# A fused attention and SwiGLU kernel: the order of its first transfers, clears and moves is changed

## The chip, the cores and the metric

The kernel runs on one core of a Trainium2 chip. The metric is the device time of one launch in microseconds (us). A core has a matrix engine (TensorE, PE in the profile, with its weight loads shown apart as PEld), VectorE (DVE), ScalarE (ACT), GpSimd (POOL) and SyncE (SP), which here only issues transfers. Each engine works through its own list of instructions in order and waits on semaphores. Transfers (DMAs) are issued from an engine's queue; SP and ACT issue all of them in this kernel.

## The reference

`x` is 2048 rows of 576 numbers in bf16. The result is `x` plus an attention branch plus a gated feed-forward branch, both fed by the same layer norm:

```python
xn = layernorm(x)                                 # over the 576 columns
q, k, v = split(xn @ wqkv)                        # 32 heads of 18 columns
s = where(0 <= i - j < 256, q @ k.T * 18**-0.5, -1e9)
attn = (softmax(s) @ v) @ wo
ffn = (silu(xn @ w1) * (xn @ w3)) @ w2            # 4608 wide
out = x + attn + ffn
```

## The kernel before

The 2048 rows are worked in four chunks (`c`) of 512. A chunk has projections (q, k, v), then 36 units (`u`), then a second stage of `w2` and `wo` products with the residual sum. A unit makes 128 of the 4608 hidden columns for the chunk's 512 rows: nine steps (`n`) of a pair of matmuls (`unit_pairs`, line 704), one for w3 and one for w1, each over 64 rows of contraction in half of the array, then a tanh on ScalarE (`unit_tanh`) and two products on VectorE (`unit_h`). Between the pairs of chunk 0's and the later chunks' units the score steps of the attention are spread (`spaced_step`, line 1020): a pair of score matmuls or more, an exp on ScalarE and masks on GpSimd. The product with v (`pv`) comes in unit 14 (for chunk 0) and later; its results are divided (`o_scale`), turned on VectorE (`o_turn`) and carried to their rows by transfers (`o_pack`, `o_rest`). `JOBS` are three pairs of PSUM banks, dealt in turn by `job()` to units, projections and `pv`: a unit's pair comes up again three deals later.

Every operation is recorded by `add` with the buffers it reads (`r`), writes first (`w`) or joins in writing (`j`); the waits between engines are worked out from these keys. Within an engine the program's order is the order of execution.

The prologue (line 809 on) loads the four x tiles of 128 rows that make chunk 0. Tiles 0 and 3 go on SP's queue, 1 and 2 on ACT's (`load_x`), then the weights of v (`wv`) and of q and k (`wa`). VectorE clears `oq` with zeros (line 821), and the zeros are multiplied by themselves on PE (`warm`, line 825), ten matmuls of 512 columns, before there is real work. Tile 0 is normalized (`ln_stats`, `ln_apart`), turned by PE into PSUM (`xn_turn`, line 399: five blocks of two 64-row halves) and moved by ScalarE into `xnT` (line 413), 640 columns at once. `proj_begin` and `proj_end` issue the two parts of a projection: a part begins with `n` = 0, 1, ... over the blocks of `xnT`. The turn of tile 1 stands between the parts of v 0, and so on. Tile 3's sum and sum of squares are taken by ScalarE (`act_sum`) instead of VectorE.

SP's queue carries, in the program's order: the first feed-forward weights (`load_w13`, six parts fill one of the slots that four units use), the swap of row halves `xnS` (`xn_swap`), four more weight parts, the key rows of head groups 0 and 1 (`span_main(0, 2)`, `span_last(0, 2)`), two transfers of query rows for groups 2 to 7 (`span_main(2, G, "sp", slice(0, 2))`), and then, unit by unit, weight parts that are owed (`owe_part`: after pairs 3, 6 and 8 of units 0 to 3, after pairs 3 and 8 later), the key rows of groups 2 to 7 in three large transfers (after unit 1), their tails (`span_last(2, G, ...)`: one after unit 2, three after unit 4, three after unit 5) and the x tiles of chunk 1 (`loads`, ahead of units 6, 8 and 17). Two of the second slot's six weight parts go on ACT's queue. The statistics of chunk 1's first tile stand on VectorE after unit 13.

All pairs of a unit name `xnS` among what they read, though only pairs 4 to 7 take their moving rows from it:

```python
src = xnT[r0:r0 + 64, c % 2, k // 2, :] if n in (0, 1, 2, 3, 8) else xnS[r0:r0 + 64, n - 4, :]
...
r=[("w13", sl), "xnS"] + xk(c), **{"j" if n else "w": [("ps", b0 + r)]})
```

Of the kernel before, what the change touches and what calls it, by code (L numbers as in the profile page):

```python
# [5 lines left out]
dt = mybir.dt  # L6
# [158 lines left out]
def bass_parallel_sum__sliding_block__glu_gated_swiglu__prompt_kernel(  # L165
# [17 lines left out]
    CH = 512  # L183
# [14 lines left out]
    with ExitStack() as es:  # L198
# [95 lines left out]
        def load_x(t, eng="sp"):  # L294
            nonlocal xp_ctr
            s = xp_ctr % NXP
            xp_ctr += 1
            add(eng, lambda e: e.dma_start(xp[s][:], x2[t * 128:(t + 1) * 128, :]), w=[("xp", s)], dma=f"xp{s}")
            return s
# [99 lines left out]
        def xn_turn(t, banks, eng="dve"):  # L399
            i = t % 2  # L400
            c, tt = divmod(t, TB)
            for k in range(5):
                for r in range(2):
                    r0 = 64 * r
                    bv = half_bank(banks[r])[:, 64 * k:64 * k + 64]
                    add("pe", lambda e, bv=bv, r0=r0, k=k: e.transpose(  # L406
                        bv, xn[i][r0:r0 + 64, k * 128:(k + 1) * 128], ident[r0:r0 + 64, r0:r0 + 64],
                        tile_position=(r0, 0)),
                        r=[("xn", i), "ident"] + ([("xnd", i)] if k == 4 else []), **{"j" if k else "w": [("ps", banks[r])]})
            both = PS[:, banks[0]:banks[0] + 2, :].bitcast(dt.bfloat16)  # L410
            src = both[:, :, 0:320].rearrange("p r (k f) -> p k r f", f=64)
            dst = xnT[:, c % 2, :, tt * 128:(tt + 1) * 128].rearrange("p k (r f) -> p k r f", f=64)
            move = (lambda e: e.tensor_copy(dst, src)) if eng == "dve" else (lambda e: e.activation(dst, src, ACT.Copy))  # L413
            add(eng, move, r=[("ps", b) for b in banks], w=[("xnT", c % 2, tt)])
# [15 lines left out]
        def xk(c):  # L430
            return [("xnT", c % 2, tt) for tt in range(TB)]
# [6 lines left out]
        def proj_part(c, what, banks, part, behind=()):  # L438
# [3 lines left out]
            for n in range(5 - part):  # L442
                for r in range(2):
# [8 lines left out]
                    elif kind == "8":  # L452
                        out_ = PS[:, banks[x], 0:CH // 2]
                        st, mv = wp[rows, kd, i, :], xnT[rows, c % 2, kd, x * (CH // 2):(x + 1) * (CH // 2)]
                        keys = ["wpr", "wp0", "wp1"] + xk(c)
                    else:
                        out_ = PS[:, banks[x], 0:HD]
                        st, mv = xnT[rows, c % 2, kd, i * 128:(i + 1) * 128], wv[rows, kd, x * HD:(x + 1) * HD]
                        keys = ["wvd" if n == 4 else f"wv{n // 2}", ("xnT", c % 2, i)]
# [195 lines left out]
        def o_scale(i):  # L655
# [5 lines left out]
                r=uq_keys[i] + ["rden", "oq0"], w=["oq"])  # L661

        def o_turn(g, half):
            i = g // 2 % NOD
            c0 = half * (CH // 2)
            add("dve", lambda e: e.transpose(od[i][:, g % 2, c0:c0 + CH // 2], oq[:, c0:c0 + CH // 2]),  # L666
                r=["oq", "oq0"], **{"j" if half or g % 2 else "w": [("od", i)]})
# [36 lines left out]
        def unit_pairs(c, u, n0, n1, b0):  # L704
# [3 lines left out]
            for n in range(n0, n1):  # L708
                for r in range(2):
# [6 lines left out]
                        r=[("w13", sl), "xnS"] + xk(c), **{"j" if n else "w": [("ps", b0 + r)]})  # L716
# [93 lines left out]
        add("act", lambda e: e.activation(sm[:, 3:4], eps[:], ACT.Sqrt), r=["eps"], w=[("sm", 3)])  # L810
        for t in (0, 3, 1, 2):
            xslot[t] = load_x(t, "act" if t > 1 else "sp")
# [8 lines left out]
        add("dve", lambda e: e.memset(oq[:].bitcast(dt.float32), 0.0), w=["oq0"])  # L821

        add("dve", lambda e: e.memset(qv[:, 0:2, :].bitcast(dt.float32), 0.0), w=[("q", g) for g in range(2)])

        def warm(b, *widths):
            for k, w in enumerate(widths):
                add("pe", lambda e, w=w: e.matmul(PS[:, b, 0:w], oq[:, 0:128], oq[:, 0:w], start=True, stop=True),  # L827
                    r=["oq0"], **{"j" if k else "w": [("ps", b)]})

        warm(4, *[CH] * 10)  # L830
# [109 lines left out]
        for what in [("q", 0), ("q", 1), ("q", 2), ("q", 3), ("8", 7), None]:  # L940
# [5 lines left out]
            elif got == ("q", 0):  # L946
                load_w13((), 4)
                span_main(0, 2, "act")
            elif got == ("q", 2):
                load_w13((), 2, "act")  # L950
# [3 lines left out]
        span_main(2, G, "sp", slice(0, 2))  # L954
# [6 lines left out]
        for c in range(NC):  # L961
# [7 lines left out]
            if c == 0:  # L969
                loads[6] = (0, 1)  # L970
# [75 lines left out]
            for u in range(NF):  # L1046
# [7 lines left out]
                for n in range(9):  # L1054
                    into = nxt - (clock + 9 - n)
                    if (u, n) == JOINT[c]:
# [24 lines left out]
                        later(u + 2, lambda g=g, ja=ja: (o_turn(g + 1, 1), o_pack(ja, "sp"), o_scale(2)))  # L1081
                        later(u + 3, lambda g=g: (o_turn(g + 2, 0), o_turn(g + 2, 1), o_scale(3)))
                        later(u + 3, lambda kept=kept: free.extend(kept))
                        later(u + 4, lambda g=g: o_turn(g + 3, 0))
                        later(u + 5, lambda g=g, ja=ja: (o_turn(g + 3, 1), o_pack(ja + 1, "sp")))
                    if (c == 0 or u or n > 1) and 9 * u + n not in calm and done < len(att) and (free or done < len(early) or done in held) and (clock >= nxt or (n == 8 and into < 3 and clock >= soon)):
# [8 lines left out]
                if u == FIRST[c]:  # L1095
# [10 lines left out]
                    later(u + 3, lambda j=j: (o_turn(2 * j + 1, 1), o_pack(j, "sp")))  # L1106
                    if j == 0:
                        for n in range(7):
                            later(u + 4 + (n if c == 0 else n // 2 + n // 6), lambda n=n: o_rest(n, "sp" if c else "act"))
# [12 lines left out]
                if c == 0 and u == 1:  # L1122
                    span_main(2, G, "act", slice(2, None))
                if c == 0 and u == 2:
                    span_last(2, G, slice(0, 1))
                if c == 0 and u in (4, 5):
                    span_last(2, G, slice(1, 3) if u == 4 else slice(3, None))
# [83 lines left out]
```

## Time and profile before

| | us |
|---|---|
| three runs | 557.55, 557.74, 560.05 |
| median | 557.74 |
| the profiled execution, its own time | 558.27 |
| the span of its instructions | 556.5 |
| TensorE's share of the span | 99% |
| granted clock over the span, as the records have it | 1.000 |

The profile is of one execution. Its busy times count work alone: issuing a transfer or waiting is not counted. A row of the timeline has the start, the time, the engine (SPq and ACTq are queues of transfers), the line of the code, the operation, and what is written from what; merged rows have a count and run from the first start to the last end. In brackets stands the idle time before it and what ended it. A row of groups has busy time and mean ns of one. A row of DMA issues has the KB of each and the median time from issue to landing; q1 is SP's queue and q10 ACT's in this kernel. A row of the chain of waits has start, time and what was on the chain. A row of stretches has the stretch, its length, each engine's busy time with its number of instructions (PE, PEld, DVE, ACT, POOL), the clock, the DMA share and GB/s.

### The profile page before, as it was taken

The numbers are of one execution on the slowest core, as the hardware profiler recorded it, in microseconds if no ns is written. First come the engines' busy times: TensorE is split into PE (matmuls) and PEld (weight loads), VectorE is DVE, ScalarE is ACT, GpSimd is POOL, SyncE is SP. The second block draws the span as 40 slices with busy tenths as digits, with TensorE's granted clock in tenths as the row PEclk, the third lists the DMA queues.
The fourth block names the chain that finished last, engine by engine and source line by source line (L and its number), as shares of the span: only waits on it lengthen the run. The fifth ranks groups of instructions, "written<-read, shape, count | busy, mean of one in ns | idle before, by whom it ended". The sixth has DMA issues, their size and how long they took to land.

```text
span 556.5 us, 15754 instructions
## 1 busy us (share of the span) xinstructions
PE 552.4 (99%) x6772; PEld 349.6 (63%) x6772; DVE 311.1 (56%) x583; ACT 259.9 (47%) x359; POOL 162.7 (29%) x385
## 2 busy tenths in 40 slices
PE   8999999999999999999999999999999999999998
PEld 4676554677654545677766544747776554455776
DVE  6466979610366888851046687874105577678211
ACT  6457766100287774700038787550005777756000
POOL 6423534300034452530003454333000334333000
PEclk9999999999999999999999999999999999999999
DMA  9986999777367459676726639677572673633652
GB/s 246 200 166 166 218 179 197 153 203 182 94 140 154 126 123 182 174 176 177 199 61 139 160 110 174 144 188 177 154 187 54 138 174 107 165 108 103 164 150 65
DMA packets 127216, 85.96 MB, mean 154 GB/s; under 512 B 34451, under 2 KB 124907, under 8 KB 127147
## 3 DMA queue, kind: packets, MB, share of 16 engines
q1 hardware_dynamic: 125107, 83.09, 64.9%
q10 hardware_dynamic: 2040, 1.87, 1.4%
q8 instruction: 53, 0.87, 0.7%
q14 instruction: 16, 0.13, 0.1%
HBM read 71.29 MB, written 2.36 MB: 132 GB/s over the span
## 4 chain that ended last, share of the span: by engine, by line
PE 99%; ACT 0%; DVE 0%; issue 0%
PE ps L713 50%; PE ps L785 25%; PE ps L461 10%; PE ps L587 6%; PE ps L644 3%; PE ps L792 3%; PE ps L827 1%; PE ps L699 0%; PE ps L406 0%; ACT xnT L413 0%; DVE ofin L803 0%; DVE oq L821 0%
## 5 line engine op out<-in xcount | busy, mean ns | idle before, releaser
L713 PE MATMUL ps<-xnT,w 64*128 64x512 bf16 x1400 | 186.2, 376 | 0.0
L713 PE MATMUL ps<-xnS,w 64*128 64x512 bf16 x1120 | 154.5, 376 | 0.0
L785 PE MATMUL ps<-w,hT 128*128 128x288 bf16 x1156 | 146.7, 286 | 0.0
L728 DVE SCALAR_TENSOR_TENSOR gs<-th,ps 128x512 bf16<-128x512 bf16 x144 | 97.8, 679 | 76.8 <-ACT th L722 75.9
L785 PEld LDWEIGHTS ps<-w,hT 128*128 128x128 bf16 x1156 | 112.5, 98 | 28.9 <-issue 0.2
L713 PEld LDWEIGHTS ps<-xnT,w 64*128 64x128 bf16 x1400 | 74.6, 94 | 58.6 <-issue 0.5
L722 ACT ACTIVATE th<-ps 128x512 bf16<-128x512 f32 x144 | 85.6, 595 | 45.1 <-PE ps L713 42.7
L731 DVE SCALAR_TENSOR_TENSOR hT<-gs,ps 128x512 bf16<-128x512 bf16 x144 | 98.9, 687 | 5.0
L713 PEld LDWEIGHTS ps<-xnS,w 64*128 64x128 bf16 x1120 | 59.7, 94 | 45.4
L596 ACT ACTIVATE pt<-ps 128x1024 bf16<-128x1024 f32 (+1 forms) x70 | 70.7, 1010 | 31.4 <-PE ps L587 31.1
L474 ACT ACTIVATE stage<-ps 128x512 bf16<-128x512 f32 x16 | 9.5, 596 | 142.0 <-PE ps L461 142.0
L623 POOL TENSOR_TENSOR hT<-hT,mk 128x128 int32<-128x128 int32 (+1 forms) x59 | 24.0, 429 | 171.4 <-ACT hT L596 171.2
L803 DVE TENSOR_TENSOR ofin<-ps,xp 128x288 bf16<-128x288 f32 x31 | 13.3, 455 | 108.3 <-PE ps L699 58.1
L623 POOL TENSOR_TENSOR pt<-pt,mk 128x128 int32<-128x128 int32 (+1 forms) x124 | 49.9, 427 | 28.8 <-ACT pt L596 28.8
L587 PE MATMUL ps<-qv,kv 64*128 64x320 bf16 (+4 forms) x528 | 53.3, 260 | 0.0
L587 PEld LDWEIGHTS ps<-qv,kv 64*128 64x128 bf16 x528 | 27.7, 94 | 26.2 <-ACT hT L596 1.5
L461 PE MATMUL ps<-xnT,wp 64*128 64x512 bf16 (+1 forms) x360 | 38.1, 355 | 0.0
L596 ACT ACTIVATE w<-ps 128x1024 bf16<-128x1024 f32 (+1 forms) x32 | 32.3, 1010 | 12.2 <-PE ps L587 12.1
L596 ACT ACTIVATE hT<-ps 128x1024 bf16<-128x1024 f32 (+1 forms) x32 | 32.3, 1009 | 5.3 <-PE ps L587 4.8
L623 POOL TENSOR_TENSOR w<-w,mk 128x128 int32<-128x128 int32 (+1 forms) x56 | 22.9, 429 | 28.7 <-ACT w L596 28.7
L666 DVE STREAM_TRANSPOSE od<-oq 128x256 bf16<-128x256 bf16 x64 | 25.8, 427 | 6.9 <-POOL oq L659 6.9
L461 PEld LDWEIGHTS ps<-xnT,wp 64*128 64x128 bf16 x360 | 18.9, 94 | 14.6 <-ACT stage L474 0.3
(93 smaller groups left out, 384.0 us busy)
## 6 DMA issues: line engine op xcount, KB each, us to landing
w<-in_B_w_dram SPq DMA_DIRECT2D x208, 192.0 KB, 4.1
w<-in_B_w_dram SPq DMA_DIRECT2D x72, 288.0 KB, 3.3
xp<-in_A_x_dram SPq DMA_DIRECT2D x30, 144.0 KB, 3.0
out_dram<-ofin SPq DMA_DIRECT2D x31, 72.0 KB, 1.7
xnS<-xnT SPq DMA_DIRECT2D x8, 256.0 KB, 4.2
oT<-od SPq DMA_DIRECT2D x40, 36.0 KB
pt<-in_A_wqkv_dram SPq DMA_DIRECT2D x4, 288.0 KB, 5.6
hT<-in_B_w_dram SPq DMA_DIRECT2D x6, 192.0 KB, 3.6
```

The source lines that it names most:

```text
L461: op = add("pe", lambda e, out_=out_, st=st, mv=mv, n=n, r0=r0, first=first: e.matmul(out_, st, mv, start=first, stop=(part == 1 and n == ...
L587: add("pe", lambda e, r0=r0, out_=out_, kb=kb, q0=q0, nb=nb: e.matmul(out_, kb4[r0:r0 + 64, g, kb + NV - NB, :] if kb < 0 else kv[r0:r0 + ...
L596: add("act", lambda e: e.activation(pt_slot(sl)[:, 0:w, :], PS[:, SC[0]:SC[1] + 1, 0:w].rearrange("p r q -> p q r"), ACT.Exp, scale=scale) ...
L623: add("pool", lambda e, vb=vb, mm=mm: e.tensor_tensor(vb, vb, mm, ALU.mult), r=(key if n == 0 else []) + ["mk"], **{"w" if n == 0 else "j" ...
L644: add("pe", lambda e, p=p, q=q, pr=pr, sl=sl, g=g, pos=pos, q0=q0, nb=nb, col=col, first=first, n=n: e.matmul(PS[32 * q:32 * q + VW, banks ...
L666: add("dve", lambda e: e.transpose(od[i][:, g % 2, c0:c0 + CH // 2], oq[:, c0:c0 + CH // 2]), r=["oq", "oq0"], **{"j" if half or g % 2 els ...
L713: op = add("pe", lambda e, n=n, r0=r0, r=r, k=k, src=src: e.matmul(PS[:, b0 + r, :], wt[r0:r0 + 64, k, fl * 128:(fl + 1) * 128], src, star ...
L722: add("act", lambda e: e.activation(th[i][:], PS[:, bg, :], ACT.Tanh, scale=0.5), r=[("ps", bg)], w=[("th", i)])
L728: add("dve", lambda e: e.scalar_tensor_tensor(out=gs[i][:], in0=th[i][:], scalar=1.0, in1=PS[:, bg, :], op0=ALU.add, op1=ALU.mult), r=[("t ...
L731: add("dve", lambda e: e.scalar_tensor_tensor(out=hT[:, u, :], in0=gs[i][:], scalar=0.5, in1=PS[:, bu, :], op0=ALU.mult, op1=ALU.mult), r= ...
L785: add("pe", lambda e: e.matmul(bank, hT[:, f, tt * 128:(tt + 1) * 128], w2[sl][:, k, n0:n1], start=first, stop=(c + 1 == NC and half == 1 ...
L792: add("pe", lambda e: e.matmul(bank, oT[:, k, tt * 128:(tt + 1) * 128], wo[:, k, d0 + n0:d0 + n1], start=False, stop=(k == 3 and (half == ...
```

## The change

- The clear of `oq` is made in two parts, 64 and 192 columns (counted as 32-bit numbers), and stands ahead of the x loads in the program. The warming matmuls wait for the first part alone and read only its columns, repeated; there are nine and a half instead of ten. The x tiles on ACT's queue wait for the second part.
- The move of tile 0's turned rows is made in two parts, blocks 0 and 1 and then 2 to 4 (new key `xnT0`); the matmuls of v 0 with `n` over 1 wait for the second part, those with `n` 0 and 1 only for the first.
- A unit's pairs wait for `xnS` only in pairs 4 to 7.
- All six weight parts of the second slot go on SP, ahead of the keys of groups 0 and 1. Queries and keys of groups 2 to 7 go on SP together after unit 3, their tails after units 4, 5 and 6, and the first x tiles of chunk 1 ahead of unit 7 instead of unit 6.
- The packs of the attention's rows (`o_pack`, `o_rest`) are each issued a unit later than before, or later in the same unit's list.
- No score step is put ahead of pair 7 of unit 22 of chunk 0; it comes at the next place where one may.

```diff
@@ -291,11 +291,11 @@
 
         xp_ctr = 0
 
-        def load_x(t, eng="sp"):
+        def load_x(t, eng="sp", behind=()):
             nonlocal xp_ctr
             s = xp_ctr % NXP
             xp_ctr += 1
-            add(eng, lambda e: e.dma_start(xp[s][:], x2[t * 128:(t + 1) * 128, :]), w=[("xp", s)], dma=f"xp{s}")
+            add(eng, lambda e: e.dma_start(xp[s][:], x2[t * 128:(t + 1) * 128, :]), r=list(behind), w=[("xp", s)], dma=f"xp{s}")
             return s
 
         nfill = 0
@@ -408,10 +408,12 @@
                         tile_position=(r0, 0)),
                         r=[("xn", i), "ident"] + ([("xnd", i)] if k == 4 else []), **{"j" if k else "w": [("ps", banks[r])]})
             both = PS[:, banks[0]:banks[0] + 2, :].bitcast(dt.bfloat16)
-            src = both[:, :, 0:320].rearrange("p r (k f) -> p k r f", f=64)
-            dst = xnT[:, c % 2, :, tt * 128:(tt + 1) * 128].rearrange("p k (r f) -> p k r f", f=64)
-            move = (lambda e: e.tensor_copy(dst, src)) if eng == "dve" else (lambda e: e.activation(dst, src, ACT.Copy))
-            add(eng, move, r=[("ps", b) for b in banks], w=[("xnT", c % 2, tt)])
+            for n, (k0, k1) in enumerate(((0, 2), (2, 5)) if t == 0 else ((0, 5),)):
+                src = both[:, :, 64 * k0:64 * k1].rearrange("p r (k f) -> p k r f", f=64)
+                dst = xnT[:, c % 2, k0:k1, tt * 128:(tt + 1) * 128].rearrange("p k (r f) -> p k r f", f=64)
+                move = (lambda e, dst=dst, src=src: e.tensor_copy(dst, src)) if eng == "dve" else (
+                    lambda e, dst=dst, src=src: e.activation(dst, src, ACT.Copy))
+                add(eng, move, r=[("ps", b) for b in banks], w=["xnT0" if n else ("xnT", c % 2, tt)])
 
         def xn_send(t):
             i = t % 2
@@ -428,7 +430,7 @@
                     r=xk(c), dma=f"xnS{n}", **{"j" if n else "w": ["xnS"]})
 
         def xk(c):
-            return [("xnT", c % 2, tt) for tt in range(TB)]
+            return [("xnT", c % 2, tt) for tt in range(TB)] + (["xnT0"] if c == 0 else [])
 
 
         def pair_of(c, i):
@@ -456,7 +458,7 @@
                     else:
                         out_ = PS[:, banks[x], 0:HD]
                         st, mv = xnT[rows, c % 2, kd, i * 128:(i + 1) * 128], wv[rows, kd, x * HD:(x + 1) * HD]
-                        keys = ["wvd" if n == 4 else f"wv{n // 2}", ("xnT", c % 2, i)]
+                        keys = ["wvd" if n == 4 else f"wv{n // 2}", ("xnT", c % 2, i)] + (["xnT0"] if c + i == 0 and n > 1 else [])
                     first = part == 0 and n == 0
                     op = add("pe", lambda e, out_=out_, st=st, mv=mv, n=n, r0=r0, first=first: e.matmul(
                         out_, st, mv, start=first, stop=(part == 1 and n == 3), tile_position=(r0, 0)),
@@ -658,13 +660,13 @@
             add("dve", lambda e: e.reciprocal(rden[:], u3[:, :, Dh]), r=uq_keys[i], w=["rden"])
             add("pool", lambda e: e.tensor_tensor(
                 o3, u3[:, :, 0:Dh], rden[:].unsqueeze(2).to_broadcast([128, CH // 32, Dh]), ALU.mult),
-                r=uq_keys[i] + ["rden", "oq0"], w=["oq"])
+                r=uq_keys[i] + ["rden", "oq0", "oq1"], w=["oq"])
 
         def o_turn(g, half):
             i = g // 2 % NOD
             c0 = half * (CH // 2)
             add("dve", lambda e: e.transpose(od[i][:, g % 2, c0:c0 + CH // 2], oq[:, c0:c0 + CH // 2]),
-                r=["oq", "oq0"], **{"j" if half or g % 2 else "w": [("od", i)]})
+                r=["oq", "oq0", "oq1"], **{"j" if half or g % 2 else "w": [("od", i)]})
 
         def o_move(eng, dst, src, key, first, sem, r):
             add(eng, lambda e: e.dma_start(dst, src), r=r, dma=sem, **{"w" if first else "j": [key]})
@@ -713,7 +715,7 @@
                     op = add("pe", lambda e, n=n, r0=r0, r=r, k=k, src=src: e.matmul(
                         PS[:, b0 + r, :], wt[r0:r0 + 64, k, fl * 128:(fl + 1) * 128], src,
                         start=(n == 0), stop=(n == 8), tile_position=(r0, 0)),
-                        r=[("w13", sl), "xnS"] + xk(c), **{"j" if n else "w": [("ps", b0 + r)]})
+                        r=[("w13", sl)] + (["xnS"] if 3 < n < 8 else []) + xk(c), **{"j" if n else "w": [("ps", b0 + r)]})
             return op
 
         def unit_tanh(u, b0):
@@ -808,8 +810,10 @@
 
         xslot = {}
         add("act", lambda e: e.activation(sm[:, 3:4], eps[:], ACT.Sqrt), r=["eps"], w=[("sm", 3)])
+        for n, (c0, c1) in enumerate(((0, 64), (64, CH // 2))):
+            add("dve", lambda e, c0=c0, c1=c1: e.memset(oq[:].bitcast(dt.float32)[:, c0:c1], 0.0), w=[f"oq{n}"])
         for t in (0, 3, 1, 2):
-            xslot[t] = load_x(t, "act" if t > 1 else "sp")
+            xslot[t] = load_x(t, "act" if t > 1 else "sp", ["oq1"] if t > 1 else [])
         for n in range(2):
             add("sp", lambda e, n=n: e.dma_start(
                 wv[:, 2 * n:2 * n + 2, :], A_wqkv[256 * n:256 * n + 256, 2 * D:3 * D].rearrange("(kd p) f -> p kd f", p=128)),
@@ -818,16 +822,14 @@
             add("act", lambda e, p=p: e.dma_start(
                 wv[64 * p:64 * p + 64, 4, p * HD:(p + 1) * HD], A_wqkv[512:576, 2 * D + p * HD:2 * D + (p + 1) * HD]),
                 dma="wvd", **{"j" if p else "w": ["wvd"]})
-        add("dve", lambda e: e.memset(oq[:].bitcast(dt.float32), 0.0), w=["oq0"])
-
         add("dve", lambda e: e.memset(qv[:, 0:2, :].bitcast(dt.float32), 0.0), w=[("q", g) for g in range(2)])
 
         def warm(b, *widths):
             for k, w in enumerate(widths):
-                add("pe", lambda e, w=w: e.matmul(PS[:, b, 0:w], oq[:, 0:128], oq[:, 0:w], start=True, stop=True),
+                add("pe", lambda e, w=w: e.matmul(PS[:, b, 0:w], oq[:, 0:128], oq[:, 0:128].unsqueeze(1).to_broadcast([128, w // 128, 128]), start=True, stop=True),
                     r=["oq0"], **{"j" if k else "w": [("ps", b)]})
 
-        warm(4, *[CH] * 10)
+        warm(4, *[CH] * 9, 256)
 
         for h in range(2):
             for n in range(2):
@@ -944,14 +946,12 @@
                 clear_keys(2, G)
                 add("pool", lambda e: e.memset(kb4[:, :, :, :].bitcast(dt.float32), 0.0), w=[("kp", g) for g in range(G)])
             elif got == ("q", 0):
-                load_w13((), 4)
+                load_w13((), 6)
                 span_main(0, 2, "act")
             elif got == ("q", 2):
-                load_w13((), 2, "act")
                 span_last(0, 2)
 
         add("act", lambda e: e.activation(th[0][:, 0:1], neghalf[:], ACT.Tanh), r=["neghalf"], w=[("th", 0)])
-        span_main(2, G, "sp", slice(0, 2))
 
         PV_COST, PV_AFTER = 6.6, 20
         FIRST = {0: 14, 1: 11, 2: 8, 3: 11}
@@ -967,7 +967,7 @@
             stat, apply, xt = ({v[k]: i for i, v in plan.items()} for k in range(3))
             loads = {8: (2,), 17: (3,)} if c + 1 < NC else {}
             if c == 0:
-                loads[6] = (0, 1)
+                loads[7] = (0, 1)
             total = 9 * NF + len(att) + 3 * PV_COST
             if c:
                 total += 9 * sum(COST[kind] for kind, _ in PROJ)
@@ -1078,12 +1078,13 @@
                         g = 2 * ja
                         later(u, lambda g=g: (o_turn(g, 0), o_turn(g, 1), o_scale(1)))
                         later(u + 1, lambda g=g: o_turn(g + 1, 0))
-                        later(u + 2, lambda g=g, ja=ja: (o_turn(g + 1, 1), o_pack(ja, "sp"), o_scale(2)))
-                        later(u + 3, lambda g=g: (o_turn(g + 2, 0), o_turn(g + 2, 1), o_scale(3)))
+                        later(u + 2, lambda g=g: (o_turn(g + 1, 1), o_scale(2)))
+                        later(u + 3, lambda g=g, ja=ja: (o_pack(ja, "sp"), o_turn(g + 2, 0), o_turn(g + 2, 1), o_scale(3)))
                         later(u + 3, lambda kept=kept: free.extend(kept))
                         later(u + 4, lambda g=g: o_turn(g + 3, 0))
-                        later(u + 5, lambda g=g, ja=ja: (o_turn(g + 3, 1), o_pack(ja + 1, "sp")))
-                    if (c == 0 or u or n > 1) and 9 * u + n not in calm and done < len(att) and (free or done < len(early) or done in held) and (clock >= nxt or (n == 8 and into < 3 and clock >= soon)):
+                        later(u + 5, lambda g=g: o_turn(g + 3, 1))
+                        later(u + 6, lambda ja=ja: o_pack(ja + 1, "sp"))
+                    if (c == 0 or u or n > 1) and (c, u, n) != (0, 22, 7) and 9 * u + n not in calm and done < len(att) and (free or done < len(early) or done in held) and (clock >= nxt or (n == 8 and into < 3 and clock >= soon)):
                         spaced_step()
                     op = unit_pairs(c, u, n, n + 1, b0[0])
                     clock += 1
@@ -1103,10 +1104,11 @@
                     later(u, lambda b=banks: (pv_out(b[0], 0), pv_out(b[1], 1), o_scale(0)))
                     later(u + 1, lambda j=j: (o_turn(2 * j, 0), o_turn(2 * j, 1), o_scale(1)))
                     later(u + 2, lambda j=j: o_turn(2 * j + 1, 0))
-                    later(u + 3, lambda j=j: (o_turn(2 * j + 1, 1), o_pack(j, "sp")))
+                    later(u + 3, lambda j=j: o_turn(2 * j + 1, 1))
+                    later(u + 4, lambda j=j: o_pack(j, "sp"))
                     if j == 0:
                         for n in range(7):
-                            later(u + 4 + (n if c == 0 else n // 2 + n // 6), lambda n=n: o_rest(n, "sp" if c else "act"))
+                            later(u + 5 + (n if c == 0 else n // 2 + n // 6), lambda n=n: o_rest(n, "sp" if c else "act"))
                 unit_h(u, b0[0])
                 for what in side.pop(u, []):
                     what()
@@ -1119,12 +1121,10 @@
                 if u in apply:
                     t = (c + 1) * TB + apply[u]
                     ln_apply(t, xslot[t])
-                if c == 0 and u == 1:
-                    span_main(2, G, "act", slice(2, None))
-                if c == 0 and u == 2:
-                    span_last(2, G, slice(0, 1))
-                if c == 0 and u in (4, 5):
-                    span_last(2, G, slice(1, 3) if u == 4 else slice(3, None))
+                if c == 0 and u == 3:
+                    span_main(2, G)
+                if c == 0 and u in (4, 5, 6):
+                    span_last(2, G, (slice(0, 1), slice(1, 3), slice(3, None))[u - 4])
                 if c == 0 and u == 13:
                     for t in range(4):
                         a0 = (4 + 14 * (t // 2)) * Dh
```

## The prediction

> **What bounds the kernel now.** I read the page first, then the chain of waits for the first 60 us.
>
> ```profile
> span 556.5 us, 15754 instructions
> PE 552.4 (99%) x6772; PEld 349.6 (63%) x6772; DVE 311.1 (56%) x583; ACT 259.9 (47%) x359; POOL 162.7 (29%) x385
> ...
> 1.24 4.39 PE ps L827 x10
> ...
> 7.01 0.79 PE ps L461 x10
> ...
> 9.79 11.71 PE ps L461 x134
> 21.50 12.95 PE ps L713 x120
> ```
>
> TensorE is busy for 552.4 of 556.5 us, so only 4.1 us of holes exist, and the chain is one run of matmuls from 9.79 us on. Whatever is saved ahead of 9.79 us moves everything after it; whatever opens a new hole later is lost. The change touches two places: the prologue (0 to 9.8 us) and the order of SP's queue (15 to 54 us). So the prologue's engines come next, VectorE's and ScalarE's rows in order of time.
>
> ```profile
> 3.51 0.46 DVE L357 BATCH_NORM_STATS2 stats<-xp 128x6 f32<-128x288 bf16 x1 [1.78 <-DMA xp<-in_A_x_dram]
> ...
> 4.49 0.41 DVE L357 BATCH_NORM_STATS2 stats<-xp 128x6 f32<-128x288 bf16 x1
> ...
> 5.13 0.43 DVE L386 TENSOR_SCALAR xn<-xp,mv,rstd 128x576 bf16<-128x576 bf16 x1
> ...
> 7.16 0.41 DVE L371 TENSOR_SCALAR xn<-xp,mv,rstd 128x512 bf16<-128x512 bf16 x1
> ...
> 6.77 0.77 ACT L860 ACTIVATE stage<-xp,sm 128x576 bf16<-128x576 bf16 x1
> ...
> 7.66 0.29 ACT L876 ACTIVATE sm<-sm,eps 128x1 f32<-128x1 f32 x1
> 8.10 0.70 ACT L413 ACTIVATE xnT<-ps 128x640 bf16<-128x640 bf16 x1
> ```
>
> VectorE is idle until tile 0 of x lands (3.51) and hardly again after that: tile 0 is normalized at 5.56 (5.13 + 0.43), tile 1 at 7.57 (7.16 + 0.41). The warming matmuls end at 5.63 (1.24 + 4.39), a tie with 5.56. Two things pace this stage: the landing of tile 0, and VectorE's own order behind it.
>
> **The clear and the warming.** Durations by form:
>
> ```profile
> L413 ACT ACTIVATE xnT<-ps 128x640 bf16<-128x640 bf16 x4 | 2.8, 703 | 1.1 <-PE ps L406 0.8
> L512 ACT ACTIVATE va<-ps 64x288 bf16<-64x288 f32 x7 | 2.8, 401 | 0.3 <-PE ps L461 0.2
> L821 DVE MEMSET oq<- 128x256 f32 x1 | 0.3, 272 | 0.9 <-PEq L1196 0.9
> L823 DVE MEMSET qv<- 128x512 f32 x1 | 0.5, 485 | 0.1
> ```
>
> A clear of 256 columns takes 272 ns and one of 512 takes 485, so 0.83 ns a column and 59 ns fixed (an estimate from these two). The first part of the clear, 64 columns, then takes 0.11 us and the second, 192, 0.22: 0.06 us more for VectorE, which is idle until 3.51 and hides it. The warming starts 0.16 us earlier, at 1.08, and is half a matmul shorter: ten took 4.39 us, so nine and a half take 4.17 and end at 5.25. That alone is worth nothing, because the first turn also needs tile 0 normalized.
>
> **ACT's two x tiles.** They wait for the second part of the clear (the clear's 0.9 us of idle and 0.33: about 1.24 us). Behind them on ACT's queue stand only the two 36 KB loads of wv.
>
> ```profile
> 0.93 0.87 ACTq L298 DMA_DIRECT2D xp<-in_A_x_dram  x2
> ...
> xp<-in_A_x_dram SPq DMA_DIRECT2D x1, 144.0 KB, 2.7
> xp<-in_A_x_dram ACTq DMA_DIRECT2D x1, 144.0 KB, 2.9
> ...
> q1 hardware_dynamic: 59, 0.07, 54.5%
> ...
> q10 hardware_dynamic: 95, 0.11, 75.0%
> q1 hardware_dynamic: 55, 0.04, 33.3%
> ```
>
> The tiles are issued from 0.93, so the wait costs tile 1 some 0.35 us: it lands at about 4.2 in place of 3.83 (0.93 + 2.9). VectorE wants it at 4.49, so that is hidden, with 0.3 us to spare. Does tile 0 gain? The last rows are the packets in the windows 2.40 to 2.75 and 2.75 to 3.15 us: in the first only SP's queue (q1) moves, in the second ACT's (q10) takes over with 95 of 150. Tile 0 has nearly all its 128 rows through before ACT's queue takes a share; so the gain is between 0 and 0.35 us (the whole delay given back). The rows lie nearer to 0; I take 0.15. [...]
>
> **The first move in two parts.** 288 columns take 401 ns and 640 take 703: 0.86 ns a column and 154 fixed. Parts of 256 and 384 columns take 0.37 and 0.48 us. The first four matmuls of v 0 may start 0.33 us sooner, the other six 0.15 us later than today (0.85 against 0.70). But what follows v 0 is the turn of tile 1, and tile 1 is normalized only at 7.57, while v 0 ends at 7.80 (7.01 + 0.79): the gain ends there, at VectorE. And ScalarE pays 0.15 us: the square sum (6.77), the root (7.66, done at 7.95) and the second move (8.10) follow. Their slack is 0.15 (7.95 to 8.10), of which about 0.1 is hand-over, so some 0.05 us comes back as a loss. The prologue's net is therefore -0.15 + 0.05 = **-0.1 us**, between +0.05 and -0.3.
>
> **SP's order.** Its queue in order of time, and what stands at the end of it:
>
> ```profile
> 24.12 4.62 SPq L322 DMA_DIRECT2D w<-in_B_w_dram  x6
> 28.79 7.60 SPq L528 DMA_DIRECT2D kv<-stage  x3
> 36.43 3.12 SPq L322 DMA_DIRECT2D hT<-in_B_w_dram  x3
> 39.59 0.83 SPq L557 DMA_DIRECT2D kv<-stage  x1
> 40.46 1.91 SPq L322 DMA_DIRECT2D hT<-in_B_w_dram  x3
> 42.42 1.26 SPq L322 DMA_DIRECT2D w<-in_B_w_dram  x2
> 43.73 2.55 SPq L557 DMA_DIRECT2D kv<-stage  x3
> 46.33 1.98 SPq L322 DMA_DIRECT2D w<-in_B_w_dram  x2
> 48.35 2.52 SPq L557 DMA_DIRECT2D kv<-stage  x3
> 50.92 0.95 SPq L298 DMA_DIRECT2D xp<-in_A_x_dram  x2
> ...
> xp<-in_A_x_dram SPq DMA_DIRECT2D x2, 144.0 KB, 2.3
> ```
>
> SP has no holes here: it runs late against the program. The x tiles of chunk 1 stand at the start of unit 6, which PE reaches near 33 us (18 matmuls a unit, and the run of 120 ends at 34.45), and are issued at 50.92. Now count what stands ahead of them. Ahead of the three large key moves (28.79) went ten weight parts on SP and two on ACT; after the change all eighteen of three fills go on SP, six more through the same DMA engines. Between the key moves and the x tiles stood ten parts; now six (units 4, 5 and 6), because the loads move from unit 6 to 7 and fall behind unit 6's two parts. The key tails number seven in both. So six parts come in at 0.77 us (4.62 / 6), +4.6, and four go out at the mean of the ten, 0.83 ((3.12 + 1.91 + 1.26 + 1.98) / 10), -3.3: x is issued at 52.2, less 0.1 for the earlier prologue. Bounds: 50.9, if the longer waits within the rows (7.60 for three, 3.12 against 1.91) shrink as much as the queue grows; 53.8, if the two parts from ACT cost SP their time as well (+8 x 0.77 - 4 x 0.83). I take 52.1, 1.2 us later.
>
> ```profile
> 53.25 0.46 DVE L357 BATCH_NORM_STATS2 stats<-xp 128x6 f32<-128x288 bf16 x1
> ...
> 54.90 0.69 DVE L731 SCALAR_TENSOR_TENSOR hT<-gs,ps 128x512 bf16<-128x512 bf16 x1
> ...
> 56.34 1.04 PE L713 MATMUL ps<-xnT,w 64*128 64x512 bf16 x8
> ```
>
> 50.92 + 2.3 is 53.2: today VectorE takes the first x tile of chunk 1 the moment it lands. 1.2 us later holds up what is queued behind it: unit 14's two products (the second ends at 55.59), which free the PSUM pair that unit 16 writes, from 56.34. The slack is 0.75 us, so PE stands for 1.2 - 0.75 = **+0.45 us** (0 to 2.15).
>
> What else the new order touches is covered. The key tail of group 2, issued at 39.59, comes behind +4.6 us of parts and one part fewer than today: about 43.4, landed by about 46 (with x's 2.3), and its scores stand here:
>
> ```profile
> 47.98 0.41 PE L587 MATMUL ps<-qv,kv 64*128 64x320 bf16 x4
> ```
>
> Two us to spare; without them every us late is a us of PE. The weights of unit 16 go out ahead of the x tiles instead of behind, which frees up to 0.1 us that counts only if x is in time. The split wait on xnS and the later packs of oT hold work back only on SP, off PE's chain. The skipped score step is taken one matmul pair later: no work changes.
>
> **Sum.** -0.1 + 0.45 = +0.35 us on this execution (558.27 us in all, 1.77 of it outside the span). It lies 0.5 above the median of the three runs, 557.74, to which I apply the difference: **558.1 us**, with its own range 557.7 to 558.6.
>
> **The rivals.**
>
> 1. *The x tiles land in time.* [...] Against: more bytes go ahead. Then -0.1 and -0.1 for unit 16's weights: 557.5.
> 2. *Tile 0 gains the whole 0.35, and x is in time.* For it: ACT's issue starts at 0.93 today, so its rows are waiting at the engines while tile 0's pass. Against: the packet rows. -0.3 - 0.1: 557.3.
> 3. *Slower: x at its upper bound.* The place is VectorE's statistics at 53.25; it decides from 0.75 us of lateness. Issued at 53.8, 2.9 us late, PE stands for 2.15 us: 557.74 - 0.1 + 2.15 = 559.8.
> 4. *The clock.* Ten warming matmuls of 512 columns took 4.39 us, 0.44 each; 60 pairs of the same width took 12.95, 0.216 a pair, so the warming ran at half rate. The shorter warming leaves a hole of 0.2 us ahead of the first turn. If full rate comes later for it, the useful work runs at half:
>
> ```profile
> 5.63:7.00 1.37, 0.91 (x13) 0.38 (x13) 1.30 (x5) 0.83 (x2) 1.09 (x4) 1.00 1.11 329
> 7.00:9.80 2.80, 2.76 (x60) 1.98 (x62) 2.37 (x9) 2.32 (x5) 1.09 (x4) 1.00 1.12 275
> ```
>
> PE is busy for 3.67 of 4.17 us there; all at half rate would be 7.3, +3.2. Half of that: 559.7. Against it: the hole of 0.46 us ahead of 7.01 (1.37 - 0.91) did no harm. [...]
>
> That the change does not do what it says (the split buys nothing) is already in the sum.
>
> **How the numbers follow.** Forecast 0.45; rival 1 0.24; rival 2 0.10; rival 3 0.12; rival 4 0.09. The range, 557.0 to 559.8, leaves out part of rivals 2, 3 and 4. 0.5% is 2.8 us, about what a measurement of this kernel can tell from no change; 560.5 is reached only past rival 3 or with two of them together: slower 0.05. 554.9 is below every case: faster 0.02. Within: 0.93.
>
> **What would show it.** Tile 0's first statistics at 3.36 in place of 3.51; two short ScalarE moves and tile 1's turn not moving by more than tile 0 did; SP's x issue near 52.1 and VectorE's statistics near 54.4, with a PE hole near 56.5. If the x issue is at 51 or before, rival 1 holds; if score matmuls of group 2 wait, the key tail was mis-costed; if PE's first 5 us stay at 0.44 us past 5.7, it is the clock.

## The result and the profile after

The median went from 557.83 us (22 runs, 557.48 to 560.05) to 559.56 us (22 runs, 557.69 to 564.52): 1.0037 times the time before, 95% interval 1.0025 to 1.0050. So the change is slower by 1.7 us where 0.35 was forecast. The spread says more than the median: the best run is 0.21 us above the best of before, and the worst nearly 7 us above that. In 10 of the 22 runs the granted clock is 0.997 or 0.994; of 104 runs of the kernel before that were timed beside the experiments, it is under 1.000 in one. The 12 runs with a whole clock have a median of 558.77, still 0.9 us above the kernel before, so the clock is not the whole loss.

The profiled execution of the changed kernel is one of the best (557.88 us, clock 1.000). It shows the mechanism, but not its usual price. First the chain of waits of its first 22 us; columns are start, time and what was on the chain.

```profile
1.66 0.45 ACTq L298
...
2.29 0.42 ACTq L822
...
2.74 5.24 DMA wv<-in_A_wqkv_dram
...
8.02 0.30 PE ps L463 x2
...
10.20 11.54 PE ps L463 x134
21.73 12.95 PE ps L715 x120
```

Before, the chain of the prologue went over PE's warming and ScalarE's move. Now it goes over ACT's queue: its second x tile (L298), behind it the loads of wv's last block (L822), and that block's landing, 5.24 us later. The first run of 120 unit matmuls starts at 21.73 where it started at 21.50. The kernel before had these rows of PE and of ACT's queue in the same stretch:

```profile
1.83 0.62 ACTq L818 DMA_DIRECT2D wv<-in_A_wqkv_dram  x1
2.48 0.61 ACTq L818 DMA_DIRECT2D wv<-in_A_wqkv_dram  x1
...
5.62 0.50 PE L406 MATMUL ps<-ident,xn 64*128 64x64 bf16 x10
...
7.63 0.43 PE L406 MATMUL ps<-ident,xn 64*128 64x64 bf16 x10
```

PE's and VectorE's timeline after the change:

```profile
1.04 4.23 PE L829 MATMUL ps<-oq 128*128 128x512 bf16 x10 [1.04 <-DVE oq L814]
5.26 0.54 PE L406 MATMUL ps<-ident,xn 64*128 64x64 bf16 x10
...
6.36 0.83 PE L463 MATMUL ps<-wv,xnT 64*128 64x288 bf16 x8
8.02 0.30 PE L463 MATMUL ps<-wv,xnT 64*128 64x288 bf16 x2 [0.83 <-DMA wv<-in_A_wqkv_dram]
8.15 0.31 PE L406 MATMUL ps<-ident,xn 64*128 64x64 bf16 x10
...
3.15 0.46 DVE L357 BATCH_NORM_STATS2 stats<-xp 128x6 f32<-128x288 bf16 x1 [1.41 <-DMA xp<-in_A_x_dram]
```

Tile 0 is there 0.36 us sooner (3.15 against 3.51), its turn starts at 5.26 in place of 5.62, and v 0 at 6.36 in place of 7.01: what the edits set out to do happens. Then PE stands for 0.83 us for wv's last block, and the turn of tile 1 begins at 8.15 instead of 7.63. The block is late for more than its issue: its second transfer was issued 0.26 us later (2.74 against 2.48), but took 5.24 us to land, where the two took 3.9 to 4.0 before. From 4.5 to 5.5 us ACT's queue moved 148 packets before, among 275 of SP's, and 17 after; after the change 155 follow from 5.5 to 7.5, among 995 of SP's queue. So the block's rows now pass among more of SP's loads; why a small delay of the issue moves them by that much, no view here shows. SP's queue and VectorE at chunk 1's first x tile:

```profile
34.22 5.92 SPq L530 DMA_DIRECT2D kv<-stage  x3
...
42.63 0.83 SPq L559 DMA_DIRECT2D kv<-stage  x1
...
51.39 1.43 SPq L298 DMA_DIRECT2D xp<-in_A_x_dram  x3
...
53.72 0.46 DVE L357 BATCH_NORM_STATS2 stats<-xp 128x6 f32<-128x288 bf16 x1 [0.35 <-DMA xp<-in_A_x_dram]
```

The x tiles are issued 0.47 us later than before, and VectorE waits 0.35 us for the first: less than the 0.75 us of slack, so PE does not stand in this execution. The two suspects are then a wait in v 0 (theory P) and the wait for x (theory S), and something that makes both dearer in other executions.

### The profile page after: what moved, and what is told of

Read it like the earlier page. It is cut to its first block, busy times and chain, and to the rows that moved or that the text cites. A ratio compares the mean times of both kernels' runs of the same rounds, so it can differ in the third digit from the quotient of the medians.

```text
span 556.2 us, 15757 instructions
## 1 busy us (share of the span) xinstructions
PE 551.7 (99%) x6772; PEld 340.1 (61%) x6772; DVE 311.0 (56%) x584; ACT 260.1 (47%) x360; POOL 163.1 (29%) x385
## 4 chain that ended last, share of the span: by engine, by line
PE 98%; DMA 1%; ACT 0%; ACTq 0%; DVE 0%; issue 0%
PE ps L715 50%; PE ps L787 25%; PE ps L463 9%; PE ps L589 6%; PE ps L646 3%; PE ps L794 3%; DMA wv<-in_A_wqkv_dram 1%; PE ps L701 0%; ACT L812 0%; ACT xnT L415 0%; ACTq L298 0%; ACTq L822 0%; PE ps L406 0%; DVE ofin L805 0%; ACT sm L812 0%
## 5 line engine op out<-in xcount | busy, mean ns | idle before, releaser
L715 PEld LDWEIGHTS ps<-xnT,w 64*128 64x128 bf16 x1400 | 70.4, 94 | 62.6 <-DVE ofin L655 0.2
L715 PEld LDWEIGHTS ps<-xnS,w 64*128 64x128 bf16 x1120 | 56.1, 94 | 48.6
```

Source lines behind the costliest of these rows:

```text
L715: op = add("pe", lambda e, n=n, r0=r0, r=r, k=k, src=src: e.matmul(PS[:, b0 + r, :], wt[r0:r0 + 64, k, fl * 128:(fl + 1) * 128], src, star ...
```

## The experiments

Times are medians; "before" is the kernel before, timed on the same chip beside the experiment: 557.86 us for e1 to e4 and for e5 to e8, 557.84 for e9 to e12, 558.11 for e13 and e14. One profiled execution per kernel stands for its trace.

**The two halves of the change.** e1_prologue has only the edits to the clear, the wait of ACT's x tiles, the split move and the warming. e2_order has only the rest.

> Only the prologue's edits (clear in two parts, ACT's x tiles wait, first move in two parts, nine and a half warming matmuls); SP's queue as before. Theory P (the loss is made in the prologue, where PE waits for the last block of wv and the clock then does not stay at full rate): median 559 to 560, spread over 3 us or more as in the changed kernel. Theory S (SP's new order loses it, by VectorE waiting for x at 54 us): 557.3 to 557.8, spread under 1 us.

> Only SP's new order, the later packs, the narrower wait on xnS and the skipped step; prologue as before. Theory P: 557.4 to 558.0, spread as before the change. Theory S: 559 to 560.

e1: 559.81 us (6 runs), ratio 1.0034 (1.0022 to 1.0047), clock under 1.000 in 3 of 6. e2: 558.68 (12 runs, up to 562.97), ratio 1.0024 (1.0006 to 1.0043), clock under 1.000 in 2 of 12. Neither theory alone: both halves lose. In e1's trace the hole in v 0 is longer, and behind it stands something new. PE's timeline, and then the busy time of each engine (PE, PEld, DVE, ACT, POOL), the clock, the DMA share and GB/s in three stretches:

```profile
7.09 0.42 PE L463 MATMUL ps<-wv,xnT 64*128 64x288 bf16 x4 [0.20 <-DMA wv<-in_A_wqkv_dram]
8.83 0.30 PE L463 MATMUL ps<-wv,xnT 64*128 64x288 bf16 x2 [1.31 <-DMA wv<-in_A_wqkv_dram]
```

```profile
6.62:10.04 3.42, 1.86 (x38) 1.00 (x34) 1.99 (x8) 1.61 (x4) 0.82 (x3) 1.00 1.13 258
10.04:13.45 3.41, 3.38 (x38) 2.19 (x40) 1.64 (x4) 2.36 (x5) 2.15 (x8) 0.50 1.10 238
13.45:16.90 3.45, 3.45 (x48) 2.08 (x46) 2.07 (x5) 2.30 (x7) 2.56 (x7) 1.00 1.14 234
```

After 3.42 us in which PE was busy for only 1.86, the clock is halved for 3.41 us, while PE has work without a pause, and then it is whole again. By an estimate, half of those 3.41 us, the drop costs 1.7 us: more than the two holes of 0.20 and 1.31 us ahead of it. There is a loss without a drop too: of e1's three runs with a whole clock two took 560.05 and 560.56 us. e2's trace has the other wait, without a drop: VectorE waits 1.97 us for x (up to 54.85 us), and PE 1.2 us for VectorE's products of unit 14 (the last row here is one of waits: us in all, times, the longest).

```profile
54.85 0.46 DVE L357 BATCH_NORM_STATS2 stats<-xp 128x6 f32<-128x288 bf16 x1 [1.97 <-DMA xp<-in_A_x_dram]
...
PE ps L713 <- DVE hT L731: 1.2, 1, 1.2
```

**Which edit of the prologue.** e3_nowait takes the wait of ACT's x tiles out of the changed kernel; e4_wvd keeps it and moves wv's last block to SP's queue.

```diff
# e3_nowait
-            xslot[t] = load_x(t, "act" if t > 1 else "sp", ["oq1"] if t > 1 else [])
+            xslot[t] = load_x(t, "act" if t > 1 else "sp")
# e4_wvd: this loop moved ahead of the loads of wv0 and wv1, and
-            add("act", lambda e, p=p: e.dma_start(
+            add("sp", lambda e, p=p: e.dma_start(
                 wv[64 * p:64 * p + 64, 4, p * HD:(p + 1) * HD],
...
```

> The changed kernel, but ACT's x tiles do not wait for the clear. Theory P1 (the wait moves wv's last block, queued behind the x tiles, and PE stands for it): wv lands by 6.6 us again, no hole of 0.8 us in v 0, median 557.3 to 557.9, tile 0 lands near 3.5 again. Theory P2 (the shorter and earlier warming costs the clock whatever lands): median stays 559 to 560.

> The changed kernel, with the last block of wv moved from ACT's queue to SP's, ahead of the rest of wv. P1: the hole in v 0 that waits for this block goes, median 557.0 to 557.8 and a small spread; the other blocks of wv may land 1 us later and open a hole of their own. P2: median 559 to 560 as the change has it. S: 559 to 560.

e3: 558.81 us (12 runs, up to 564.20; ratio 1.0024, 1.0004 to 1.0044). Its trace has no wait for wv and tile 0 again at 3.41 us, as theory P1 has it, but its runs still spread, and the expected 557.3 to 557.9 was missed. SP's new order is still in it; its own profiled execution, 557.77 us, is one of its best and has no wait for x (issued at 50.21, taken at 52.77), so that x makes the spread is shown only by e6_both below. e4: 560.54 (ratio 1.0046, 1.0028 to 1.0063), no better than the change, where 557.0 to 557.8 was expected. Its profiled execution, 563.04 us, is the clearest picture of theory S, the wait for x. PE's timeline, then the stretches:

```profile
55.84 0.38 PE L715 MATMUL ps<-xnT,hT 64*128 64x512 bf16 x2
59.65 1.59 PE L715 MATMUL ps<-xnT,w 64*128 64x512 bf16 x8 [3.43 <-DVE hT L733]
```

```profile
56.20:59.65 3.45, 0.02 (x3) 0.03 (x2) 2.42 (x6) 1.14 (x2) 1.25 (x4) 1.00 0.62 178
60.00:63.40 3.40, 3.40 (x24) 1.66 (x20) 3.37 (x10) 1.02 (x1) 2.15 (x5) 0.50 1.09 234
63.50:67.00 3.50, 3.50 (x40) 2.03 (x38) 2.54 (x5) 2.67 (x4) 1.80 (x5) 1.00 0.97 205
```

Here x was issued at 53.20 and VectorE waited for it until 57.17 (4.17 us); PE stood 3.43 us at unit 16, and from 60.00 to 63.40 us the clock is 0.50: 3.43 + 1.7 (half of 3.40, an estimate) is 5.1 of the 5.2 us that this execution lies above 557.86.

**Taking the waits away, one and both.** The x tiles go out ahead of unit 3 in e5_xearly (changed kernel), e6_both (e3_nowait) and e7_orderx (e2_order); e8_fill puts five idle matmuls into e1_prologue's v 0.

```diff
-                loads[7] = (0, 1)
+                loads[3] = (0, 1)
# e8_fill, in proj_part
             for n in range(5 - part):
+                if (c, what, part, n) == (0, ("v", 0), 0, 4):
+                    warm(3, *[CH] * 5)
```

> The changed kernel, but the first x tiles of chunk 1 go out ahead of unit 3 instead of unit 7, so VectorE never waits for them at 53 us. Theory S alone (all of the loss is that wait): median 557.2 to 557.8. Theory P alone (all of it is the prologue): 559.5, as the change. Both: the loss of the prologue alone is left, about 559 to 560 with no run's VectorE waiting for x.

> The changed kernel with x of chunk 1 ahead of unit 3 and without the wait of ACT's x tiles. If the two waits (wv's last block in v 0, x at 53 us) are the whole loss: 557.3 to 557.9, spread under 1.5 us, no run with a clock under 1. If the shorter warming costs the clock by itself: 558.5 or more, some runs under 1.

> SP's new order alone (prologue as before), with x of chunk 1 ahead of unit 3. Theory S: the tail of e2_order to 563 goes, median 557.5 to 557.9. If something else in the new order loses (the key tails, the packs): it stays near 558.7.

> The prologue's edits alone, with five more warming matmuls put between blocks 3 and 4 of v 0, where PE waits for wv's last block. If the hole costs its length alone: no better than e1_prologue (559.8), since PE cannot go on before wv lands, and worse by up to 1 us where wv is in time. If the hole also makes the clock fall back for a stretch: fewer runs under 1, median 558 to 559.

| kernel | ACT's x tiles wait | x of chunk 1 behind unit 6's parts | median us (range) | ratio, 95% interval | clock under 1.000 |
|---|---|---|---|---|---|
| changed | yes | yes | 559.56 (557.69 to 564.52) | 1.0037, 1.0025 to 1.0050 | 10 of 22 |
| e5_xearly | yes | no | 559.32 (557.90 to 561.75) | 1.0022, 1.0010 to 1.0034 | 6 of 12 |
| e3_nowait | no | yes | 558.81 (557.77 to 564.20) | 1.0024, 1.0004 to 1.0044 | 2 of 12 |
| e6_both | no | no | 558.09 (557.31 to 559.38) | 1.0005, 0.9995 to 1.0014 | 1 of 11 |
| e2_order | no | yes | 558.68 (557.84 to 562.97) | 1.0024, 1.0006 to 1.0043 | 2 of 12 |
| e7_orderx | no | no | 558.00 (557.67 to 559.52) | 1.0003, 0.9995 to 1.0012 | 0 of 11 |

With both causes gone no loss is left that can be told from none, nor the long spread; nor is there a gain. The wait of ACT's tiles is worth 1.2 us (559.32 - 558.09) with its clock drops, the late x 0.7 in the median (558.81 - 558.09, and 558.68 - 558.00), and of these six only kernels with the late x have runs above 562. The two do not add up exactly (1.2 + 0.7 against 559.56 - 558.09 = 1.5): each median stands on 11 to 22 runs that spread by microseconds. What remains of the change in e6_both (the split move, the shorter warming, the narrow wait on xnS, the later packs and the eighteen weight parts in a row) makes no difference that these runs can tell (ratio 0.9995 to 1.0014). e8_fill answered nothing: in its profiled execution the wait came ahead of the inserted matmuls (0.87 us for another block of wv), and 559.67 us (7 runs) with one run under 1.000 is no clear step from e1's 559.81.

**A hole put in, and two mends that failed.** e11_late is e6_both with wv's last block put behind the first two loads of wqk on SP. e10_wvd1 and e12_between are e5_xearly with that block in one transfer, after or between ACT's x tiles. e9_before_x is the kernel before with x early.

```diff
# e10_wvd1, e12_between (there behind ACT's first x tile); v's matmuls read the block at these columns
-            add("act", lambda e, p=p: e.dma_start(
-                wv[64 * p:64 * p + 64, 4, p * HD:(p + 1) * HD], A_wqkv[512:576, 2 * D + p * HD:2 * D + (p + 1) * HD]),
+        add("act", lambda e: e.dma_start(
+            wv[:, 4, 0:HD], A_wqkv[512:576, 2 * D:3 * D].rearrange("r (p f) -> p r f", p=2)),
# e9_before_x
-                loads[6] = (0, 1)
+                loads[3] = (0, 1)
```

> The kernel before, with x of chunk 1 ahead of unit 3 instead of unit 6. Its VectorE took that tile the moment it landed. If some of its runs above 558.5 are VectorE waiting for x: median 557.5 to 557.8 and a smaller spread. If not: the same as before, 557.86.

> The changed kernel with x early (as e5_xearly) and wv's last block loaded by one transfer on ACT's queue instead of two, so that its end is issued 0.6 us sooner. Theory P (the second of the two transfers lands late behind the x tiles): the wait of 0.8 us shrinks to 0.2 or less, median 558.0 to 558.6 against e5's 559.32. If wv as a whole lands too late for a v 0 that starts at 6.4 us: little change, 559.

> The kernel of e6_both (no wait, x early, 558.09) with wv's last block made late on purpose, behind the first two loads of wqk on SP. A hole of 2 to 3 us opens in v 0. If a hole costs its own length alone: 560 to 561, all clocks 1.000, a small spread. If the clock falls back after it: 561 to 563, most runs under 1.000, a half-rate stretch behind the hole in the trace.

> As e10_wvd1, but with that one transfer between ACT's two x tiles. It is issued near 1.65 us, where the changed kernel's last one goes near 2.75. Theory P: no wait for this block in v 0; tile 2 lands 0.5 us later, still by 5.8. Median 557.4 to 558.2, and if tile 0's gain of 0.36 us survives the rest of wv, under the kernel before.

e9: 558.26 us, ratio 1.0008 (0.9999 to 1.0016): the kernel before loses nothing that can be measured by its tie at 53.2 us. e11: 560.27 (9 runs, 1.0048), clock under 1.000 in 7 of 9; the hole in its profiled execution was 1.40 us, shorter than planned, and that execution, at 558.80 and a whole clock, one of the two best. What holes the seven runs with a drop had, no view shows. e10 and e12 made the wait longer instead of shorter: 561.59 and 562.19 us (5 runs each), and every one of the ten runs has a clock under 1.000. In e10 PE waited 2.90 us for that one transfer; the stretches of e10 follow the row:

```profile
10.22 0.30 PE L463 MATMUL ps<-wv,xnT 64*128 64x288 bf16 x2 [2.90 <-DMA wv<-in_A_wqkv_dram]
```

```profile
7.30:10.70 3.40, 0.49 (x15) 0.41 (x16) 1.03 (x5) 0.50 (x3) 0.57 (x1) 1.00 1.12 266
10.70:14.10 3.40, 3.40 (x46) 2.39 (x44) 1.55 (x4) 2.09 (x4) 2.55 (x8) 0.50 0.47 133
14.20:17.60 3.40, 3.40 (x50) 2.27 (x48) 2.33 (x5) 2.73 (x7) 1.55 (x7) 1.00 0.97 219
```

In e12 the wait for the block was 1.14 us. Tile 2 of x, now behind it on ACT's queue, was issued at 2.86 us instead of 1.66, and ACT's two x tiles took 4.6 us to land in the median, where the changed kernel's took 3.1. The statistics of tile 2 stand on VectorE ahead of the `xn` for which PE then stood 1.82 us more:

```profile
8.75 0.29 PE L463 MATMUL ps<-wv,xnT 64*128 64x288 bf16 x2 [1.14 <-DMA wv<-in_A_wqkv_dram]
...
10.87 0.46 PE L406 MATMUL ps<-ident,xn 64*128 64x64 bf16 x10 [1.82 <-DVE xn L371]
```

As mends they failed; as tests of the clock they are the strongest. With some 3 us of holes in the profiled execution (2.90 in e10, 1.14 and 1.82 in e12) all ten runs have a clock under 1.000. With shorter waits for wv the count has no clear order: 1.40 us (e11) seven of nine, 1.31 (e1) three of six, 0.87 (e8) one of seven, 0.84 (e5) six of twelve, 0.60 (e14, below) five of twelve, with one profiled execution each. No threshold is shown. In e13's profiled execution (clock 0.997; its run is below) eight matmuls of v take 1.14 us from 8.49 on, where e4's take 0.66 from 8.02; PE's rows add up to 2.05 busy us in the 3.41 ahead of that. In e11's (clock 1.000) such eight keep to 0.67 us at 9.26, with 1.94 busy us in the 3.41 from 6.90 to 10.31; but the stretches of 3.41 us that meet in its hole, at 7.81 us, have about 2.85 and 2.25, so the share depends on where a stretch begins.

Why e10's one transfer, issued at 2.14 us, held PE until 10.22 is not shown: the views have its lateness alone.

**The wait alone.** e14_waitonly is the kernel before with its one clear put ahead of the x loads, and ACT's x tiles waiting for it. e13_wvd_x is e4_wvd with x early.

```diff
# e14_waitonly, on the kernel before; the clear of oq stands ahead of this
-            xslot[t] = load_x(t, "act" if t > 1 else "sp")
+            xslot[t] = load_x(t, "act" if t > 1 else "sp", ["oq0"] if t > 1 else [])
```

> The kernel before with nothing but the wait of ACT's x tiles for the clear of oq. If the wait alone makes the prologue's loss: wv's last block lands near 7.5 or later, PE waits for it in v 0, median 558.7 to 559.8, some runs under 1.000. If it takes the split move or the shorter warming as well: 557.7 to 558.2.

> The kernel of e4_wvd (wv's last block on SP ahead of the rest of wv) with x of chunk 1 ahead of unit 3. The waits of 3.4 us at unit 16 go; left are two waits of 0.4 to 0.5 us in v 0. Against tile 0's gain of 0.36 us that is near nothing: 557.8 to 558.6. If the wait costs the clock however small the holes are: 559 or more, with runs under 1.000.

e14: 558.97 us against 558.11 (ratio 1.0025, 1.0012 to 1.0037), clock under 1.000 in 5 of 12 runs, and in PE's timeline the same two matmuls waiting:

```profile
8.23 0.30 PE L461 MATMUL ps<-wv,xnT 64*128 64x288 bf16 x2 [0.60 <-DMA wv<-in_A_wqkv_dram]
```

So the wait makes a loss by itself, about 0.9 us; neither the split move nor the shorter warming is needed for it. e13: 558.67 (1.0008, 0.9996 to 1.0019), 3 of 12 under 1.000: with the block on SP's queue the loss cannot be told from none, but PE waits 0.91 and 0.36 us for wv in its profiled execution, where 0.4 to 0.5 each was expected. It is e4 with x early and nothing else, and the two intervals (1.0028 to 1.0063 and 0.9996 to 1.0019) do not meet: here the late x costs clear of noise, while in the pairs of the table above the intervals overlap. No version was found that beats both kernels.

## Why the prediction was wrong, step by step

- **The step that failed** is the paragraph on ACT's two x tiles: "Behind them on ACT's queue stand only the two 36 KB loads of wv." They were named and given no price. They were issued at 1.83 and 2.48 before, and the block landed by 6.5 (2.48 + 4.0); after, they were issued from 2.14, and it landed at 7.98, when v 0, started 0.65 us sooner, had used up the other blocks. The price is 0.83 us of hole in the profiled execution, 1.31 in e1's, and 0.9 us of median for the wait alone (e14); in the changed kernel the wait is worth 1.2 us (e5 against e6), where the prediction had the whole prologue at -0.1. The same delay was priced for tile 1, with 0.3 us to spare, and there it held: in the profiled execution VectorE does not wait for that tile.
- **The clock** was rival 4, with the wrong cause and too small a chance (0.09). The prediction put it on the shorter warming; the runs put it on the holes. It also took the hole of 0.46 us ahead of 7.01 as evidence against the clock. In the trace before, the stretches of 3.4 us from 3.60, 4.20, 5.63 and 6.55 us on, which all hold that hole, have PE busy for 2.90 to 2.94 us; the clock fell after 1.86 of 3.42 us (e1), 0.49 of 3.40 (e10) and 0.02 of 3.45 (e4). What share is enough is not shown. That the change moves the clock is shown: 10 of its 22 runs are under 1.000, against 1 of 104 of the kernel before. What decides which of the 22 is not shown.
- **The x tiles of chunk 1** were the right mechanism: issue, VectorE's statistics, unit 14's products, PE at unit 16 (PE's wait of 3.43 us in e4 names VectorE's product). The size for the median was fair, 0.45 us against 0.7, but in part by luck, since it stood for one execution. The profiled execution alone says otherwise: issued at 51.39, not 52.1, and VectorE's wait of 0.35 us inside the slack of 0.75, so rival 1 held there; the three large key moves took 5.92 us in place of 7.60. What was missed is that one trace gives one point: VectorE waited for the same tile 1.97 us in e2 and 4.17 in e4, where it came 3.9 us later than before the change (57.17 against 53.25), past the 2.9 of rival 3.
- **Tile 0's gain** was taken as 0.15 of 0.35 us by the packets of both queues; it is 0.36. "Nearly all" of tile 0's 128 rows were 90 packets by 2.75 us, and the lead arises ahead of that: by 2.40 us SP's queue had moved 31 packets before and 89 after, when ACT's had moved none before and 2 after. With ACT's tiles held, the first statistics start at 3.01 to 3.21 us in the profiled executions of eight kernels; with no hold at 3.36 to 3.70 in those of six and at 3.51 in the kernel before. e14, held by the one large clear, has 3.36, so what exactly ACT's queue takes from tile 0, ahead of any packet of its own, stays open.
- **The split move** behaved as costed (two moves in 0.76 us), started v 0 sooner, and bought nothing. The prediction saw it hidden behind VectorE's tile 1; in fact the landing of wv, at 7.98 us, came later still. Its 0.1 us of hand-over was an estimate; the trace before has 0.14 from ScalarE's first move (ends 6.87) to v 0 (7.01) and 0.06 from VectorE's tile 0 (5.56) to PE's turn (5.62).
- **The key tail** was right: predicted at about 43.4, issued at 42.63, and no score matmul of group 2 waits in this execution.
- "Within 0.5%" came true (1.0037), and the median lies in the range, at its upper end; but the likeliest value, 558.1, was 1.5 us low. The upper end stands for x alone being late (rival 3); that the median lies inside with the wait for wv, which no rival has, is luck.

## What to carry to other kernels

Before a transfer is delayed, list what is queued behind it on the same queue, with the moment each of these is wanted: here two loads of 36 KB behind two tiles cost 0.83 us of wait, more than the 0.36 us that tile 0 gained. Weigh holes of the matrix engine by more than their length: in e1, e4 and e10 a stretch of 3.40 to 3.45 us in which PE was busy for 1.86, 0.02 and 0.49 us was followed by 3.40 to 3.41 us at a clock of 0.50, by an estimate (half of that) another 1.7 us each; in e11, with a hole of 1.40 us, the clock stayed at 1.000. And where a transfer lands the moment it is wanted, take its time from several executions: a tie in one trace can be a wait in another.

## What the runs showed of the hardware that was not expected

- A stretch at a clock of 0.50 deep in the kernel (60.00 to 63.40 us in e4), after one that PE stood through (0.02 busy us of 3.45), as in the prologue (10.04 to 13.45 in e1, after 1.86 of 3.42).
- A start of ACT's queue some 0.14 us after SP's (0.93 against 0.79) goes with a later landing of SP's first tile: VectorE takes it at 3.51 us, and at 3.15 with ACT held back until 1.23; but at 3.36 in e14, held until 1.22.
- The same transfer at nearly the same moment takes very different times: with x issued at 53.20 (e4) it was taken at 57.17, 4 us later, where 2.3 us were enough in the kernel before (50.92 to 53.25), in the changed one (51.39 to 53.72) and in e2 (52.60 to 54.85). Each is one execution of its own kernel; what made e4's slow is open.
